# Strassen's identity in the first expert layer of the last two token chunks

## The chip, the cores and the metric

The kernel runs on one core of a Trainium2 chip. Its engines work side by side, each through its own queue of instructions in the order in which the program issues them: TensorE (PE: matmuls, with its weight loads listed as PEld), VectorE (DVE), ScalarE (ACT), GpSimd (POOL) and SyncE (SP, which only issues transfers). Engines wait for each other through semaphores. The metric is the device time of one execution in microseconds (us); lower is better. The time is a median over runs; the profile is of one further execution.

## The reference

An attention over 8 batches and 8 heads (576 queries of 64 numbers, and 16 beacon keys ahead of the 576 keys) is followed by a two-layer network on all 8 x 576 = 4608 tokens:

```python
scores = scale * np.matmul(q, k_all.transpose(0, 1, 3, 2))
scores = np.where(causal, -1000000000.0, scores)
a = np.exp(scores - scores.max(-1, keepdims=True))
a /= a.sum(-1, keepdims=True) + 1e-09
attn = np.matmul(a, v_all)
x = np.ascontiguousarray(attn.transpose(0, 2, 1, 3)).reshape(B * S, H * D)   # 4608 x 512
h = x @ w_in                      # 512 x 2048
g = np.maximum(0.01 * h, h)
out = (g @ w_out).astype(np.float32)   # 2048 x 512
```

## The kernel before

All instructions of the five engines stand in the order in which the Python code issues them (`tc.manual_schedule`); the framework adds the semaphore waits that the data and the buffers need.

**Attention.** Work goes by groups `g`, one for each pair of heads of a batch: 32 of them. A group has score matmuls (`score`, `stretch`, L314), exponentials on ACT (L329, L333), triangular masks on POOL (L289), value matmuls in two halves (`value`, L359), and a division on DVE (L388, L389) into `x_nat`. For groups 8 and on `x_turn` (L412) then issues transposes on SP's queue, which carry `x_nat` into `xT`, the tokens laid out with their 512 features over partitions. In the last batch `x_turn` issues three of them: L417, L422 and, last, L425 with the first 112 tokens of the batch. `xT` holds four batches at a time.

**The two layers.** Tokens go by chunks of 512, nine of them (`NCH`). Chunk 7 takes most of its tokens from batch 6 and its last 64 from batch 7; chunk 8 is all of batch 7. `moe1` computes 128 columns of the first layer for a chunk: four matmuls of 512 columns (L442) and one ACT instruction that applies the leaky ReLU into `gT` (L450). `up` does that once and keeps the count `done1`; there are 16 for a chunk.

The second layer already uses Strassen's identity in Winograd's form, on halves of the tokens, of the hidden features and of the output columns: seven products in the order `PRODUCTS = (1, 4, 6, 2, 7, 5, 3)`, each over two tiles of 128 tokens. `moe2` (L524) is one such tile, called a group here: 8 matmuls of 256 columns (L537). `down` does one group and keeps `at2` and `done2`; there are 14 for a chunk. `combine` (L556) puts the products together: products 1, 4 and 5 are copied from the bank by ACT (L568), the others are added by DVE (L565), and four blocks are stored by SP (L595). The sums of `gT` that the identity needs are made by DVE from `token_sums` (L469): two slices with four sums each. They wait in the list `due`, and `up` and `down` take one from it each time (`add_due`, L620).

**Order.** While attention runs, a list of `events` with due times places the attention's steps, and `fill` places `up` and `down` between them so that the work at hand is spread evenly up to the end of a batch; `KEPT` = 4 units are kept back. After the last event the loop at L836 runs what is left: the rest of chunk 6's groups, then all of chunk 7's first layer, then chunk 8's first layer and chunk 7's groups by turns, then chunk 8's 14 groups.

**PSUM.** The eight banks are divided into a pool of four single ones (`ps_one`, used by `moe1`, `moe2`, the value matmuls and a third of the score tiles) and a pool of two pairs (`ps_sc`, used by score tiles alone).

The step that matters for the change in the first layer is this:

```python
acc = ps_one.tile([128, 512], FP32, name="acc", tag="one")
...
nc.scalar.activation(out=gT[i][:, fc, :], in_=acc, func=AF.Prelu, alpha=0.01)
```

## Time and profile before

| | |
|---|---|
| runs | 326.14 us median of 3 (325.81 to 326.32) |
| profiled execution | 325.23 us, of it span 323.5 us |
| granted TensorE clock | 0.999 |
| PE busy | 317.3 us |
| DVE busy | 146.1 us |
| ACT busy | 199.3 us |
| first-layer matmuls (L442) | 640 recorded, 135.7 us |
| end of the last value matmuls | 257.6 us |
| chunk 7's first layer | 268.1 to 281.9 us |
| chunks 8 and 7 by turns | 281.9 to 308.0 us |
| chunk 8's second layer | 308.0 to 320.2 us |

The span runs from the program's first to its last recorded instruction; the rest of the execution's time lies around it. A line of the timeline gives the start and the length in us, the engine, the line of the kernel, the operation with its output and input, how many instructions were merged, and in brackets how long the engine was idle before and what ended that. Merged matmuls overlap, so their length is not their count times one. A line of the chain of work gives start, length, engine, tile and line.

### The profile page before, as it was taken

The page shows a single profiled execution, that of the slowest core. Times are in us where ns is not written, and L with a number is a line of the kernel's source. Part 1 is how long each engine was busy: PE and PEld are TensorE (multiplying, and loading weights), DVE is VectorE, ACT ScalarE, POOL GpSimd, SP SyncE. Part 2 cuts the span into 40 slices and gives each one's busy share as a digit, 9 for nine tenths or more (in the row PEclk, how much of TensorE's full clock was granted, in tenths as well). Part 3 has the DMA queues.
Part 4 walks back from the last instruction along what each step waited for, and adds up shares of the span by engine and source line. Part 5 has one row for each costly group of instructions (what it writes and reads, how often), then busy time and mean ns, then how long its engine had stood idle before and what let it go on. Part 6 is the DMA issues. An engine that isn't in the chain of part 4 may idle for free.

```text
span 323.5 us, 8521 instructions
## 1 busy us (share of the span) xinstructions
PE 317.3 (98%) x3429; PEld 213.4 (66%) x3429; DVE 146.1 (45%) x297; ACT 199.3 (62%) x336; POOL 184.7 (57%) x354
## 2 busy tenths in 40 slices
PE   8999999999999999999999999999999999999995
PEld 5574565445687558845888888656865785466684
DVE  3473354518446145434552455345444542325444
ACT  4969862487765786478647873786468415653420
POOL 8895968999997687659875977664221000000000
PEclk9999999999999999999999999999999999999999
DMA  8999999999999999999999999999112112000203
GB/s 140 137 206 175 147 214 120 188 165 190 157 138 169 218 147 107 124 174 80 154 192 160 110 127 115 196 128 135 52 53 79 24 54 97 2 1 32 79 20 132
DMA packets 155928, 39.93 MB, mean 123 GB/s; under 512 B 143040, under 2 KB 153152, under 8 KB 155888
## 3 DMA queue, kind: packets, MB, share of 16 engines
q0 software_dynamic: 99824, 18.54, 91.3%
q1 hardware_dynamic: 55792, 20.77, 37.1%
q8 instruction: 27, 0.44, 0.6%
q14 instruction: 13, 0.11, 0.1%
q10 hardware_dynamic: 272, 0.07, 0.1%
HBM read 37.22 MB, written 9.44 MB: 144 GB/s over the span
## 4 chain that ended last, share of the span: by engine, by line
PE 77%; DMA 10%; POOL 5%; ACT 3%; DVE 2%; issue 2%; DVEq 0%; POOLq 0%; ACTq 0%
PE acc L442 31%; PE acc L537 30%; PE av L359 6%; PE sc L314 6%; DMA w_out_sb<-in_moe_w_out_dram 4%; PE acc L512 4%; DMA w_in_sb<-in_moe_w_in_dram 4%; POOL aT L289 2%; DMA gsum<-in_k_dram 2%; ACT aT L333 2%; POOL gsum L158 2%; ACT aT L329 1%; DVE p L565 0%; ACT gT L450 0%; DVE u L565 0%
## 5 line engine op out<-in xcount | busy, mean ns | idle before, releaser
L442 PE MATMUL acc<-xT,w_in_sb 128*128 128x512 bf16 (+1 forms) x640 | 135.7, 358 | 0.3 <-ACT aT L329 0.3
L450 ACT ACTIVATE gT<-acc 128x512 bf16<-128x512 f32 x144 | 82.8, 621 | 46.4 <-PE acc L442 46.2
L442 PEld LDWEIGHTS <-w_in_sb 128*128 128x128 bf16 x640 | 59.6, 98 | 52.4 <-issue 2.9
L289 POOL TENSOR_SCALAR_AFFINE_SELECT aT<-aT 128x256 bf16<-128x256 bf16 (+2 forms) x160 | 59.7, 404 | 51.7 <-ACT aT L329 30.9
L537 PEld LDWEIGHTS <-gT 128*128 128x128 bf16 x512 | 48.8, 98 | 9.1 <-issue 1.8
L333 ACT ACTIVATE aT<-sc 128x1024 bf16<-128x1024 f32 (+3 forms) x64 | 51.8, 895 | 0.0
L537 PE MATMUL acc<-w_out_sb,gT 128*128 128x256 bf16 x384 | 46.2, 273 | 0.4 <-ACT gT L450 0.4
L329 ACT ACTIVATE aT<-sc 128x512 bf16<-128x512 f32 (+3 forms) x64 | 29.0, 522 | 27.9 <-PE sc L314 27.7
L388 DVE RECIPROCAL rec<-av 128x6 f32<-128x6 f32 (+1 forms) x64 | 12.0, 188 | 67.0 <-PE av L359 66.3
L359 PEld LDWEIGHTS <-aT 128*128 128x128 bf16 (+1 forms) x960 | 36.7, 98 | 8.3 <-issue 0.6
L537 PEld LDWEIGHTS <-gsum 128*128 128x128 bf16 x384 | 36.5, 98 | 6.2 <-issue 0.4
L359 PE MATMUL av<-v_aug,aT 128*128 128x65 bf16 (+1 forms) x960 | 39.4, 194 | 0.3 <-ACT gT L450 0.2
L214 POOL DMA_DIRECT2D v_aug<-in_v_dram x40 | 34.2, 859 | 4.1 <-DMA w_in_sb<-in_moe_w_in_dram 3.4
L568 ACT COPY p<-acc 128x512 f32<-128x512 f32 (+1 forms) x25 | 14.5, 580 | 35.6 <-PE acc L537 35.6
L171 POOL DMA_DIRECT2D k_nat<-in_k_dram x48 | 34.9, 733 | 1.3 <-DMA w_out_sb<-in_moe_w_out_dram 0.6
L171 POOL DMA_DIRECT2D q_nat<-in_q_dram x48 | 34.8, 731 | 0.6 <-issue 0.3
L389 DVE TENSOR_TENSOR x_nat<-av,rec 128x384 bf16<-128x384 f32 (+1 forms) x64 | 31.4, 491 | 2.2
L537 PE MATMUL acc<-w_sum,gsum 128*128 128x256 bf16 x256 | 31.9, 273 | 0.0
L276 ACT ACTIVATE aT<-sc 128x1024 bf16<-128x1024 f32 (+3 forms) x32 | 25.9, 875 | 3.5 <-PE sc L267 3.5
L620 DVE TENSOR_TENSOR gsum<-gT 128x1024 bf16<-128x1024 bf16 x16 | 11.0, 688 | 28.1 <-ACT gT L450 28.1
L314 PE MATMUL sc<-qT,kT 64*128 64x80 bf16 (+22 forms) x384 | 22.0, 250 | 0.3
L314 PEld LDWEIGHTS <-kT 64*128 64x128 bf16 x384 | 12.9, 94 | 10.9 <-issue 7.6
(62 smaller groups left out, 227.3 us busy)
## 6 DMA issues: line engine op xcount, KB each, us to landing
out_dram<-p SPq DMA_DIRECT2D x26, 256.0 KB, 3.2
q_nat<-in_q_dram POOLq DMA_DIRECT2D x48, 72.0 KB, 5.5
k_nat<-in_k_dram POOLq DMA_DIRECT2D x48, 72.0 KB, 5.0
v_aug<-in_v_dram POOLq DMA_DIRECT2D x24, 128.0 KB, 6.1
w_in_sb<-in_moe_w_in_dram POOLq DMA_DIRECT2D x2, 1024.0 KB, 11.7
w_out_sb<-in_moe_w_out_dram POOLq DMA_DIRECT2D x2, 1024.0 KB, 11.7
out_dram<-u SPq DMA_DIRECT2D x8, 256.0 KB, 2.7
gsum<-in_q_dram POOLq DMA_DIRECT2D x8, 144.0 KB, 6.9
```

Source lines behind the costliest of these rows:

```text
L171: nc.gpsimd.dma_start(out=t[:, :, par], in_=(q, k)[which][b, 2 * hp + par].rearrange("(t p) d -> p t d", p=NR),)
L214: nc.gpsimd.dma_start(out=dst[lo : ROWS[c], c, :, 0:D], in_=v[b, :, OFF[c] : OFF[c] + n].rearrange("h p d -> p h d"),)
L276: nc.scalar.activation(out=aT[:, :, c0 : c0 + w], in_=sc[:, :, 0:w], func=AF.Exp, scale=0.125)
L289: nc.gpsimd.affine_select(out=view, in_=view, compare_op=ALU.is_ge, fill=0.0, base=128 - n if lo == 0 else 0, channel_multiplier=-1, patte ...
L314: nc.tensor.matmul(out=(sc[par] if apart else sc[:, par])[:, at : at + b - a], lhsT=kT[ps_, c * 128 : (c + 1) * 128], rhs=qT[ps_, q0 : q0 ...
L329: nc.scalar.activation(out=probs[g][:, par, lo:hi], in_=sc[par][:, at : at + hi - lo], func=AF.Exp, scale=0.125)
L333: nc.scalar.activation(out=probs[g][:, :, lo:hi], in_=sc[:, :, at : at + hi - lo], func=AF.Exp, scale=0.125)
L359: nc.tensor.matmul(out=avv[:, n, 0 : D + 1], lhsT=aT[0 : ROWS[c], par, a0 : a0 + 128], rhs=va[0 : ROWS[c], c, 2 * hp + par, :], start=(c = ...
L389: nc.vector.tensor_tensor(out=x_nat[:, t0:t1].rearrange("p t e d -> p (t e) d"), in0=avv[:, :, 0:D], in1=rec[:, n0:n1, None].to_broadcast( ...
L442: nc.tensor.matmul(out=acc[:, lo:hi], lhsT=w_in_cols(fc, j), rhs=xT[:, j, x0 : x0 + hi - lo], start=(j == 0), stop=(j == NJ - 1), skip_gro ...
L450: nc.scalar.activation(out=gT[i][:, fc, :], in_=acc, func=AF.Prelu, alpha=0.01)
L537: nc.tensor.matmul(out=acc[:, lo : lo + HD], lhsT=left(i, n, fc, tile), rhs=right(n, fc), start=(lo == 0 and fc == 0), stop=(fc == HF - 1) ...
```

## The change

In the last two chunks (7 and 8) three quarters of the first layer are computed with the same identity: tokens, features and hidden columns are halved, and the 12 column blocks are taken in three rounds (`ROUNDS`), each of four blocks. A round (`in_round`) is seven products in the order 1, 4, 6, 5, 2, 7, 3, each of four matmuls of 256 columns; it takes the four banks of `ps_one`. Product 2 accumulates on product 1's bank, 7 on 6's, 3 on 5's, after the earlier product has been read: product 1 by an ACT copy into `p1`, product 6 by DVE's addition `u2`, product 5 by an ACT copy into `p5`. DVE then adds `u3`, `c21`, `c12` and `c22`, and the function `leave` inside the round is the ACT instruction that applies the leaky ReLU, from a bank for the first block and from SBUF for the other three. The remaining four column blocks of each chunk are done by `up` as before.

The sums of weights (`w_in_sums`, eight DVE instructions in all) and of tokens (`x_in_sums`, four for a chunk) go through `due`. They and the partial results lie in buffers that attention has finished with: `a_bufs`, the keys' buffer `k_all`, and part of `w_in_sb`.

The order changes too. The last group's `finish` comes one unit earlier, and `LEFT` = 14 groups of chunk 6 are kept back instead of 4 units, so that none of them is done before the last value matmuls. After the events stands an order written by hand (`last_chunks`: d a group, r a round, u a plain block, a that many entries of `due`, x the sums of a chunk's tokens put into `due`, t the same for the first slice of `gT`): seven groups of chunk 6 come before the first round, and single groups or pairs between the rounds. There the second layer takes its banks from `ps_sc` (one of each pair) instead of `ps_one`.

```diff
@@ -450,6 +450,13 @@
         nc.scalar.activation(out=gT[i][:, fc, :], in_=acc, func=AF.Prelu, alpha=0.01)
 
     HF, HD, HT = NF // 2, DM // 2, 256
+    TAIL, ROUNDS = NCH - 2, 3
+    apart_from_values = [False]
+
+    def one_bank():
+        if apart_from_values[0]:
+            return ps_sc.tile([128, 2, 512], FP32, name="sc", tag="sc")[:, 0]
+        return ps_one.tile([128, 512], FP32, name="acc", tag="one")
     ADD, SUB = ALU.add, ALU.subtract
 
     def weight_sums(part):
@@ -530,7 +537,7 @@
         n, tile = PRODUCTS[n2 // 2], n2 % 2
         apart = i == NCH - 1 and n2 >= 10
         if tile == 0 or apart:
-            banks["p"] = ps_one.tile([128, 512], FP32, name="acc", tag="one")
+            banks["p"] = one_bank()
         acc = banks["p"]
         lo = 0 if apart else tile * HD
         for fc in range(HF):
@@ -597,6 +604,122 @@
             in_=c.rearrange("p (t d) -> p t d", t=n),
         )
 
+    flat_a = [t.rearrange("p e c -> p (e c)") for t in a_bufs]
+    flat_k = k_all.rearrange("p n c -> p (n c)")
+    W_COLS, X_COLS, T_COLS = 2 * 256 * ROUNDS, 2 * HT, 1024
+    w_t = {n: flat_a[i][:, 0:W_COLS].rearrange("p (j f) -> p j f", j=2) for i, n in enumerate((5, 6, 4))}
+    w_t[7] = w_in_sb[1][:, 0:2, 0 : W_COLS // 2]
+    sum_at = [(i, W_COLS + n * X_COLS) for i in range(3) for n in range(3)]
+    temp_at = [(flat_k, n * T_COLS) for n in range(5)] + [(flat_a[3], n * T_COLS) for n in (1, 2)]
+    temps = {
+        name: t[:, lo : lo + T_COLS].bitcast(FP32)
+        for name, (t, lo) in zip(("p1", "p5", "u2", "u3", "c12", "c21", "c22"), temp_at)
+    }
+
+    def w_in_sums(n):
+        (b11, b21), (b12, b22) = (
+            [w_in_sb[i][:, lo : lo + 2, 0 : W_COLS // 2] for lo in (0, 2)] for i in range(2)
+        )
+        x, y = {5: (b12, b11), 6: (b22, w_t[5]), 4: (b21, w_t[6]), 7: (b22, b12)}[n]
+        due.extend((TAIL - 1, dict(out=w_t[n][:, j], in0=x[:, j], in1=y[:, j], op=SUB)) for j in range(2))
+
+    def x_parts(i):
+        at = i * 512 % (XR * S)
+        assert at + 512 <= XR * S
+        return [[xT[:, 2 * c : 2 * c + 2, at + r * HT : at + (r + 1) * HT] for c in range(2)] for r in range(2)]
+
+    x_sums = {}
+
+    def x_in_sums(i):
+        (a11, a12), (a21, a22) = x_parts(i)
+        s1, s2, s3, s4 = (
+            flat_a[t][:, lo : lo + X_COLS].rearrange("p (j t) -> p j t", j=2)
+            for t, lo in sum_at[4 * (i - TAIL) : 4 * (i - TAIL) + 4]
+        )
+        x_sums[i] = {5: s1, 6: s2, 7: s3, 3: s4}
+        return [
+            (i, dict(out=s1, in0=a21, in1=a22, op=ADD)),
+            (i, dict(out=s2, in0=s1, in1=a11, op=SUB)),
+            (i, dict(out=s4, in0=a12, in1=s2, op=SUB)),
+            (i, dict(out=s3, in0=a11, in1=a21, op=SUB)),
+        ]
+
+    def in_product(i, n, r, bank, first):
+        (a11, a12), (_, a22) = x_parts(i)
+        x = {1: a11, 2: a12, 4: a22}.get(n)
+        x = x_sums[i][n] if x is None else x
+        for f in range(2):
+            cols = slice(r * 256 + f, r * 256 + f + 255, 2)
+            for j in range(2):
+                if n in w_t:
+                    w = w_t[n][:, j, cols]
+                else:
+                    i0, j0 = {1: (0, 0), 2: (0, 2), 3: (1, 2)}[n]
+                    w = w_in_sb[i0][:, j0 + j, cols]
+                nc.tensor.matmul(
+                    out=bank[:, f * HT : (f + 1) * HT],
+                    lhsT=w,
+                    rhs=x[:, j],
+                    start=first and f == 0 and j == 0,
+                    stop=j == 1,
+                    skip_group_check=True,
+                )
+
+    def in_round(i, r):
+        if i not in gT:
+            gT[i] = gpool.tile([128, NF, 512], BF16, name="gT")
+        b = [ps_one.tile([128, 512], FP32, name="acc", tag="one") for _ in range(4)]
+        add = nc.vector.tensor_tensor
+
+        def leave(half, cols, src):
+            fc = cols * HF + 2 * r
+            nc.scalar.activation(
+                out=gT[i][:, fc : fc + 2, half * HT : (half + 1) * HT],
+                in_=src.rearrange("p (f t) -> p f t", f=2),
+                func=AF.Prelu,
+                alpha=0.01,
+            )
+
+        in_product(i, 1, r, b[0], True)
+        nc.scalar.copy(out=temps["p1"], in_=b[0])
+        in_product(i, 4, r, b[3], True)
+        in_product(i, 6, r, b[1], True)
+        add(out=temps["u2"], in0=b[1], in1=temps["p1"], op=ADD)
+        in_product(i, 5, r, b[2], True)
+        nc.scalar.copy(out=temps["p5"], in_=b[2])
+        in_product(i, 2, r, b[0], False)
+        leave(0, 0, b[0])
+        in_product(i, 7, r, b[1], False)
+        add(out=temps["u3"], in0=b[1], in1=temps["p1"], op=ADD)
+        add(out=temps["c21"], in0=b[3], in1=temps["u3"], op=ADD)
+        leave(1, 0, temps["c21"])
+        in_product(i, 3, r, b[2], False)
+        add(out=temps["c12"], in0=b[2], in1=temps["u2"], op=ADD)
+        leave(0, 1, temps["c12"])
+        add(out=temps["c22"], in0=temps["u3"], in1=temps["p5"], op=ADD)
+        leave(1, 1, temps["c22"])
+        done1[0] += 4
+
+    def last_chunks(steps):
+        for step in steps.split():
+            op, n = step[0], int(step[1:] or 1)
+            i = done1[0] // NF
+            if op == "d":
+                for _ in range(n):
+                    down()
+            elif op == "u":
+                for _ in range(n):
+                    up()
+            elif op == "r":
+                for _ in range(n):
+                    in_round(i, done1[0] % NF // 4)
+            elif op == "x":
+                due.extend(x_in_sums(n))
+            elif op == "a":
+                add_due(n)
+            elif op == "t":
+                due.extend((i, op) for op in token_sums(i, 0, SLICE))
+
     done1, done2, at2, ready, turn, first_down, held = [0], [0], [0, 0], [0], [0], [0], [0]
 
     def fill(rest=False):
@@ -671,7 +794,7 @@
             )
 
     NG = B * NPAIR
-    KEPT, LEAD = 4, 4
+    KEPT, LEAD, LEFT = 4, 4, 14
 
     def has(g):
         return 0 <= g < NG
@@ -811,9 +934,12 @@
             events.append((FIRST + (0.4 if m else 0.6) + 1536 / COLS * m, 2, block, (m,)))
         ends = [FIRST]
         for g in range(FIRST, NG):
-            events.append((g + 3.5, 2, finish, (g, 2)))
+            at = g + (2.5 if g == NG - 1 else 3.5)
+            events.append((at, 2, finish, (g, 2)))
             if g % NPAIR == NPAIR - 1:
-                ends.append(g + 3.5)
+                ends.append(at)
+        for at, n in ((NG - 1.2, 5), (NG - 0.3, 6), (NG + 0.7, 4)):
+            events.append((at, 7, w_in_sums, (n,)))
         for b in range(2, B):
             for n in range(2 if b == 2 else 0, NKB):
                 events.append((4 * b + ((-0.1, 0.1)[n > 3] if b == 2 else 0.3 * n - 0.4), 6, load_v_cast, (b, n)))
@@ -823,7 +949,7 @@
         for at, _, what, args in events:
             while w + 2 < len(ends) and at > ends[w + 1]:
                 w, d0 = w + 1, done1[0] + done2[0]
-            todo = NF * ready[0] + sum(ND(i) for i in range(ready[0])) - KEPT - d0
+            todo = NF * ready[0] + sum(ND(i) for i in range(ready[0])) - (KEPT if w + 2 < len(ends) else LEFT) - d0
             aim = d0 + todo * (at - ends[w]) / (ends[w + 1] - ends[w])
             while done1[0] + done2[0] < aim and fill():
                 pass
@@ -833,8 +959,12 @@
                 while done1[0] + done2[0] < since + (2 if has_down() else 4) and fill(True):
                     pass
             what(*args)
-        while at2[0] < NCH:
-            fill()
+        assert at2 == [TAIL - 1, ND(TAIL - 1) - LEFT] and done1[0] == TAIL * NF, (at2, done1)
+        apart_from_values[0] = True
+        w_in_sums(7)
+        due.extend(x_in_sums(TAIL))
+        last_chunks("d7 a9 r d2 x8 r d2 t r d1 u4 d2")
+        last_chunks("d2 a9 r d2 r d2 t r d2 u4 d6 d14")
 
 
 # ---- launch: one core; inputs and outputs as the reference has them ----
```

## The prediction

> **What bounds the kernel now.** I read the page's busy line first, then the chain of work that ended last in order of time, then the timeline of the last 75 us, then the groups by shape. The page:
>
> ```profile
> PE 317.3 (98%) x3429; PEld 213.4 (66%) x3429; DVE 146.1 (45%) x297; ACT 199.3 (62%) x336; POOL 184.7 (57%) x354
> ```
>
> TensorE (PE) is busy for 317.3 of 323.5 us. The chain, in order of time, shows the part that the change rewrites:
>
> ```profile
> 257.64 10.48 PE acc L537 x96
> 268.12 13.81 PE acc L442 x64
> ...
> 307.97 8.75 PE acc L537 x80
> 316.74 0.70 DVE u L565
> ```
>
> From 257.64 to 316.74 it is on PE without a break: nothing else counts while PE never waits. The rows price a matmul: 10.48 / 96 = 109.2 ns for 256 columns, 13.81 / 64 = 215.8 ns for 512. What else is needed comes from the timeline:
>
> ```profile
> 266.41 0.58 ACT L568 COPY p<-acc 128x512 f32<-128x512 f32 x1 [6.40 <-PE acc L537]
> 267.03 0.69 DVE L565 TENSOR_TENSOR u<-u,p 128x512 f32<-128x512 f32 x1 [0.89 <-ACT p L568]
> 267.75 0.69 DVE L565 TENSOR_TENSOR p<-u,p 128x512 f32<-128x512 f32 x1
> ...
> 276.42 0.69 DVE L620 TENSOR_TENSOR gsum<-gsum,gT 128x1024 bf16<-128x1024 bf16 x1
> 277.03 0.68 DVE L620 TENSOR_TENSOR gT<-gT 128x1024 bf16<-128x1024 bf16 x1
> 277.63 0.69 DVE L620 TENSOR_TENSOR gsum<-gT,gsum 128x1024 bf16<-128x1024 bf16 x1
> ...
> 286.12 1.03 PE L442 MATMUL acc<-xT,w_in_sb 128*128 128x512 bf16 x4
> 286.76 0.97 PEld L537 LDWEIGHTS <-gT 128*128 128x128 bf16 x8
> 286.98 1.04 PE L537 MATMUL acc<-w_sum,gT 128*128 128x256 bf16 x8
> 287.18 0.60 ACT L450 ACTIVATE gT<-acc 128x512 bf16<-128x512 f32 x1 [1.14 <-PE acc L442]
> ```
>
> A VectorE (DVE) addition follows one whose result it needs 0.72 us after (267.03 to 267.75), one that it does not need 0.61 after (276.42, 277.03, 277.63). A reader of a bank starts 0.20 us after PE's last matmul there has made way for the next group (286.98 to 287.18). ScalarE (ACT) hands over 0.04 after its end (266.99 to 267.03). Back to back, ACT takes 0.51:
>
> ```profile
> 245.55 2.12 ACT L450 ACTIVATE gT<-acc 128x512 bf16<-128x512 f32 x4
> ```
>
> (2.12 - 0.60) / 3. From SBUF in float32 the groups by shape have one row:
>
> ```profile
> L760 ACT CAST k_nat<-gsum 64x576 bf16<-64x576 f32 x1 | 0.7, 672 | 0.2 <-DMA gsum<-in_k_dram 0.2
> ```
>
> Scaled to 512 elements that is about 0.62, so a leave from SBUF costs what one from PSUM does. Last, the transposes into xT of the last pair of heads:
>
> ```profile
> 258.34 1.20 SPq L417 DMA_TRANSPOSE xT<-x_nat  x1
> 259.59 1.24 SPq L422 DMA_TRANSPOSE xT<-x_nat  x1
> 260.87 1.74 SPq L425 DMA_TRANSPOSE xT<-x_nat  x1
> ```
>
> ```profile
> DMA to landing us min/median/max: 2.3/2.4/2.9
> ```
>
> The second fence is the answer for L425. The third transpose carries the 64 tokens that chunk 7 lacks; it is issued 3.4 us after the last value matmul (257.5) and lands 2.3 to 2.9 later. Before, 12.2 us of groups stood ahead of chunk 7, so it hid.
>
> [...]
>
> **The change part by part.** *Removed:* in six rounds, 16 matmuls of 512 columns (3.45 us) give way to 28 of 256 (3.06 us): 0.40 each, **2.4 us off PE**. The 14 groups of the second layer per chunk are as many as before.
>
> *Added on DVE and ACT:* per round five float32 additions (u2, u3, c21, c12, c22) in place of none, and six ACT instructions in place of four. A chunk then has 22 float32 additions and 8 sums of gT at 0.61 and 4 sums of x at 0.34, some 19.7 us of DVE against 3 x 3.06 + 3.45 + 14 x 0.874 = 24.9 us of PE. ACT has 18 + 4 + 3 at 0.51, 12.8 us. Load alone costs nothing; what costs is order, because PE now returns to banks that DVE or ACT must have read. Products 2, 7 and 3 accumulate where 1, 6 and 5 lie: product 2 waits for the copy of product 1 (ACT), product 7 for u2 (DVE), which itself needs that copy.
>
> *Standard case* (round 1 to 2 of chunk 7), from the end of product 7 of the earlier round. DVE: u3 0.20, c21 0.92, c12 1.53, c22 2.14, seen 0.72 later at 2.86. ACT's queue is in order, so the new round's copy of product 1 stands behind the leave of c22: leave 2.86, copy 3.37, done 3.99. PE meanwhile does product 3 (0.44), two groups (1.75) and products 1, 4, 6, 5 (1.75), and wants product 2 at 3.93: late 0.06. u2 runs 3.99 to 4.71; PE wants product 7 at 4.37: **late 0.34** in all.
>
> *Round 2 to 3, chunk 7:* behind c22 DVE has a sum of x (2.75), the second layer's u (3.09) and p (3.81), another sum (4.42), then u2 at 4.76, ready 5.48 against 4.37: **1.11**.
>
> *Round 3 to chunk 8's round 1:* c22 2.14, two sums of x to 3.43. The next addition needs the copy of p5, which stands in ACT's queue behind the leave of c22: 3.37, done 3.99. From there two additions (3.99, 4.71), four sums of gT (5.32, 6.04, 6.65, 7.26), then 7.87, the product 3 addition 8.48, sums 9.09, 9.70, 10.31, u2 10.92, ready 11.64. PE: product 3 0.44, a group 0.87, four plain columns 3.45, four groups 3.49, five products 2.18, product 7 at 10.43: **1.21**.
>
> *Chunk 8, round 1 to 2:* the second layer's copy of p4 stands ahead of the copy of product 1 on ACT: done 4.50, product 2 late 0.57, u2 ready 5.22: **0.85**. *Round 2 to 3:* standard, **0.34**.
>
> *Chunk 7, round 1* is moved up: seven groups (6.1 us) stand between the last value matmul and it. The third transpose lands at 5.8 to 6.3 after that matmul; the first sum of x waits for it on DVE, with the second layer's u2 and three sums queued behind it: sum 5.9, u2 6.24, sum 6.85, seen at 7.31; PE wants product 6 at 6.99, late 0.32, and product 7 another 0.1: **0.4**, or 0.9 with the late landing.
>
> *At nothing:* the eight sums of w_in run under attention and the first groups (0.55 us each, estimated as for x), with DVE at 45%; two banks for the second layer instead of four suffice, since a pair of groups lasts 1.75 us and its reader 0.20 + 0.7; uncovered, the last four single groups could lose 0.05. Later stores on SP hold nobody until the last, whose tail after PE (additions, store) is unchanged.
>
> *Sum:* 0.4 + 0.34 + 1.11 + 1.21 + 0.85 + 0.34 = 4.25 of new waits, less 2.41 = **+1.8**, rounded to +1.9 with the last banks. The profiled execution took 325.23 us with a span of 323.5; its span would become 325.4. The median of the runs is 0.9 above that execution: 326.14 + 1.9 = **328.0 us**.
>
> **Bounds of what the trace does not show.** Sums of 512 bfloat16: 0.2 to 0.5 spacing, four on PE's path, -0.5 to +0.6; I take 0.34. Leave from SBUF: 0.60 to 0.67, +0.3 at most. Weights loaded from every second column under a matmul of 256: L442 loads such columns only under 512; its loads average 98 ns, like L537's contiguous ones, which do fit in 109. Zero is taken, 20 ns each on 168 matmuls (3.4 us) is the upper end. A gain below nothing has no source there.
>
> **Rivals.** *(a) Faster:* DVE drains its queue sooner than 0.61 per addition. About 32 additions and sums stand in the chains above, so 2.0 us of waiting less, 0.06 each (0.55 spacing), makes the change even, and 0.085 makes it 0.65 faster; with no waits at all 323.7. For it: DVE's total of 19.7 fits in 24.9. Against: each spacing is measured on the same shapes. *(b) No change:* half the waits go, the two long ones at chunk 8's start and round 3 being met by slack in sums that are off the path: 326.1. *(c) Much slower:* alternate-column weight loads or a late landing add 2 us or more: 330 to 332. Against: the 98 ns. That the change does not save its 2.4 is excluded by the counts of matmuls.
>
> **How the numbers follow.** My forecast, 326.8 to 329.5, gets 0.62; (c) 0.14; (b) 0.10; (a) 0.14. Runs of before spread over 0.5 us, so 0.2% (0.65 us) is about what can be told from nothing: faster 0.14, same 0.10, slower 0.76. The range reaches down to 325.4, past (b), and up to 330.0, some way into (c), leaving out about 2 in 10.
>
> **What would show it.** PE idle of 4 to 5 us between the last value matmul and the end, ended by DVE's u2 and ACT's copy at products 7 and 2, longest (about 1.2) at chunk 8's first round and chunk 7's third; product matmuls at 109 ns. DVE nearly without gaps from c22 to u2 there. Wrong would be: no such idle (a), matmuls slower than 109 ns (c), or product 4 waiting for a transpose by over 1 us.

## The result, and the profile after

The changed kernel took 330.11 us in the median of six runs, the kernel before 325.83; the ratio is 1.0123, with a 95% interval of 1.0084 to 1.0161. In a second series beside the experiments it was 329.53 against 326.33, a ratio of 1.0088 (1.0057 to 1.0120). It is slower, by 3 to 4 us. Medians are over all runs; the ratios leave out the runs in a slower state that either kernel shows now and then, one of these six. The profiled execution took 330.05 us with a span of 328.1. The busy line of its page:

```profile
PE 316.4 (96%) x3501; PEld 220.0 (67%) x3501; DVE 170.2 (52%) x343; ACT 204.7 (62%) x348; POOL 185.7 (57%) x354
```

TensorE (PE) is busy 0.9 us less than before and the span is 4.6 us longer; DVE has 46 instructions and 24 us more. The waits between 245 us and the end (columns: who waited for whom, total us, times, longest us) name the causes:

```profile
DVE aT L743 <- DMA xT<-x_nat: 3.1, 1, 3.1
...
PE acc L659 <- DVE kT L687: 1.9, 2, 1.0
...
PE acc L659 <- DVE aT L743: 0.9, 1, 0.9
...
PE acc L659 <- DMA xT<-x_nat: 0.6, 1, 0.6
...
PE acc L659 <- ACT kT L684: 0.4, 1, 0.4
```

L659 is a product's matmul, L687 is u2, L684 the copy of product 1, L743 a sum that was due. The chain that ended last (start, us, what) ran on PE without a break before. Now it comes to the first round of chunk 7 by way of the transposes and DVE:

```profile
258.92 1.23 SPq L422
260.15 0.04 issue
260.19 4.02 DMA xT<-x_nat
...
264.58 0.68 DVE u L572
265.26 0.34 DVE aT L743
265.61 0.04 issue
265.65 2.06 PE acc L659 x16
```

It is the third transpose, 4.02 us under way; its view by source line has this answer:

```profile
DMA to landing us min/median/max: 2.3/2.4/4.0
```

Before, the same line read 2.3/2.4/2.9. The timeline at that place and at the three longest seams behind it:

```profile
263.35 0.27 PE L659 MATMUL acc<-xT,aT 128*128 128x256 bf16 x1
...
264.24 0.43 DVE L743 TENSOR_TENSOR aT<-xT 128x512 bf16<-128x512 bf16 x1 [3.13 <-DMA xT<-x_nat]
264.26 0.49 PE L659 MATMUL acc<-xT,aT 128*128 128x256 bf16 x3 [0.63 <-DMA xT<-x_nat]
...
265.65 0.60 PE L659 MATMUL acc<-aT,aT 128*128 128x256 bf16 x4 [0.91 <-DVE aT L743]
...
278.23 1.03 PE L659 MATMUL acc<-aT,w_in_sb 128*128 128x256 bf16 x8 [0.86 <-DVE kT L687]
...
290.26 1.03 PE L659 MATMUL acc<-aT,w_in_sb 128*128 128x256 bf16 x8 [0.99 <-DVE kT L687]
...
295.19 0.60 PE L659 MATMUL acc<-xT,w_in_sb 128*128 128x256 bf16 x4 [0.40 <-ACT kT L684]
```

The brackets are the idle time that a releaser ended, counted to the modelled end of the last matmul; the first matmul of a row keeps its slot of 109 ns, so I take a wait from start to start, less 109 ns for each matmul between. In round 1 that is 0.80 us at product 4, which waits for the landing (263.35 to 264.26), 1.06 at product 6, which waits for a sum of x, and 0.14 at product 7. By site, beside the forecast and a second execution of the same kernel (a1 below), in us:

| Site | Forecast | After | After, again |
|---|---|---|---|
| Chunk 7, round 1 | 0.4 | 2.00 | 0.34 |
| Chunk 7, round 1 to 2 | 0.34 | 0.43 | 0.43 |
| Chunk 7, round 2 to 3 | 1.11 | 1.11 | 1.10 |
| Round 3 to chunk 8 | 1.21 | 1.16 | 1.16 |
| Chunk 8, round 1 to 2 | 0.85 | 0.85 | 0.85 |
| Chunk 8, round 2 to 3 | 0.34 | 0.36 | 0.36 |
| Last banks | 0.05 | 0.07 | 0.07 |
| Sum | 4.30 | 5.98 | 4.31 |

**The start-up.** Of the 4.6 us between the two spans, 1.0 us lies ahead of any changed instruction. One group of 18 value matmuls, ahead of the tail in every kernel, serves as a mark. In PE's timelines of the kernel before, the same kernel again (b1 below), and the changed one:

```profile
236.84 0.72 PE L359 MATMUL av<-v_aug,aT 128*128 128x65 bf16 x18
```

```profile
239.06 0.72 PE L359 MATMUL av<-v_aug,aT 128*128 128x65 bf16 x18
```

```profile
237.85 0.72 PE L359 MATMUL av<-v_aug,aT 128*128 128x65 bf16 x18
```

Two executions of one and the same program reach the mark 2.2 us apart, so 1.0 us there says nothing about the change. From here on I use the time from the mark to the end of the span, which leaves the start-up out: 86.66 before, 90.25 after. The difference, 3.6 us, is 5.98 of waits less the 2.41 of saved TensorE work. (The views give the span to 0.1 us, so each of these times can be off by 0.05.)

### The profile page after: what moved, and what is told of

It reads as the page before. It is cut to its first block, busy times and chain, and to the rows that moved or that the text cites. A ratio compares the mean times of both kernels' runs of the same rounds, so it can differ in the third digit from the quotient of the medians.

```text
span 328.1 us, 8750 instructions
## 1 busy us (share of the span) xinstructions
PE 316.4 (96%) x3501; PEld 220.0 (67%) x3501; DVE 170.2 (52%) x343; ACT 204.7 (62%) x348; POOL 185.7 (57%) x354
## 4 chain that ended last, share of the span: by engine, by line
PE 76%; DVE 8%; ACT 6%; DMA 4%; POOL 3%; issue 2%; SPq 1%; ACTq 0%; POOLq 0%; DVEq 0%
PE acc L442 29%; PE acc L544 19%; PE av L359 9%; PE sc L544 6%; PE sc L314 6%; PE acc L519 3%; DMA v_aug<-in_v_dram 3%; PE acc L659 2%; ACT aT L333 2%; DVE gsum L743 1%; ACT gT L676 1%; PE sc L267 1%; DMA xT<-x_nat 1%; POOL gsum L158 1%; POOL v_aug L214 1%
## 5 line engine op out<-in xcount | busy, mean ns | idle before, releaser
L442 PE MATMUL acc<-xT,w_in_sb 128*128 128x512 bf16 (+1 forms) x544 | 113.0, 354 | 0.7 <-ACT aT L276 0.4
L289 POOL TENSOR_SCALAR_AFFINE_SELECT aT<-aT 128x256 bf16<-128x256 bf16 (+2 forms) x160 | 60.6, 408 | 50.6 <-ACT aT L329 30.8
L450 ACT ACTIVATE gT<-acc 128x512 bf16<-128x512 f32 x120 | 68.1, 625 | 28.1 <-PE acc L442 27.9
L442 PEld LDWEIGHTS <-w_in_sb 128*128 128x128 bf16 x544 | 50.1, 98 | 44.2 <-issue 3.5
L544 PE MATMUL acc<-w_out_sb,gT 128*128 128x256 bf16 x240 | 28.9, 273 | 0.4 <-ACT gT L450 0.4
L544 PE MATMUL acc<-w_sum,gsum 128*128 128x256 bf16 x160 | 20.1, 273 | 0.0
L575 ACT COPY p<-acc 128x512 f32<-128x512 f32 x15 | 9.1, 604 | 16.8 <-PE acc L544 16.8
L743 DVE TENSOR_TENSOR gsum<-gT 128x1024 bf16<-128x1024 bf16 x16 | 11.0, 688 | 15.3 <-ACT gT L450 15.3
```

Of the source, the lines that this page charges most:

```text
L289: nc.gpsimd.affine_select(out=view, in_=view, compare_op=ALU.is_ge, fill=0.0, base=128 - n if lo == 0 else 0, channel_multiplier=-1, patte ...
L442: nc.tensor.matmul(out=acc[:, lo:hi], lhsT=w_in_cols(fc, j), rhs=xT[:, j, x0 : x0 + hi - lo], start=(j == 0), stop=(j == NJ - 1), skip_gro ...
L544: nc.tensor.matmul(out=acc[:, lo : lo + HD], lhsT=left(i, n, fc, tile), rhs=right(n, fc), start=(lo == 0 and fc == 0), stop=(fc == HF - 1) ...
```

## The experiments

My theory: the matmuls saved are real and the loss is waits, each set by the order of the queues of DVE and ScalarE, with the landing of the third transpose on top. Rivals: the rearrangement itself costs; the start-up does; DVE is simply full. The waits of all runs below are taken from start to start, as in the table.

**e1, the order alone.** Each Strassen round gives way to four plain blocks; groups ahead, separate banks and order stay.

```diff
-        w_in_sums(7)
-        due.extend(x_in_sums(TAIL))
-        last_chunks("d7 a9 r d2 x8 r d2 t r d1 u4 d2")
-        last_chunks("d2 a9 r d2 r d2 t r d2 u4 d6 d14")
+        last_chunks("d7 a9 u4 d2 u4 d2 u4 d1 u4 d2")
+        last_chunks("d2 a9 u4 d2 u4 d2 u4 d2 u4 d6 d14")
```

(The earlier sums of w_in are left out too.)

> The order of the changed kernel kept (seven second-layer groups ahead, value banks apart), but each Strassen round replaced by four plain first-layer blocks, and no sums of weights or of x. My theory (the loss is the waits of the rounds, 6.0 us, less 2.4 us of TensorE work saved): TensorE work is that of the kernel before, and the only wait in the tail is the first plain block of chunk 7 for the third transpose, 1.3 us if it lands as late as in the changed kernel (4.0 us after issue), 0 if it lands after 2.4 us; so 0 to 1.3 us over the kernel before in the profiled execution. Rival (the rearrangement itself, pools apart and groups moved ahead, costs what was lost): 3 to 4 us over the kernel before, with waits at the places of the order and not of the sums. Start-up theory (the 1.0 us of extra idle time before 80 us is scatter of an execution): it is there or not there without regard to the tail.

Measured: 86.82 us from mark to end, level with the 86.66 and 86.74 of the two profiles of before; PE waits 0.07 us in the tail, at the last banks, and the view of waits has no row of PE there. The rearrangement costs nothing in the tail; what is lost belongs to the rounds. The transpose landed 2.4 us after issue here, to which I come back. In 18 runs against 52 the ratio is 1.0026 (1.0006 to 1.0046), some 0.8 us that this profile's tail does not show; its mark stood 0.34 us late. That remainder is not explained.

**a1 and b1, both kernels again.** No edit.

> The changed kernel once more, beside the others. My theory: the waits in the tail behind round 1 are the same to 0.05 us (0.43, 1.11, 1.16, 0.85, 0.36), since they come from queues; the landing of the third transpose is late again, since TensorE's fetches fall at the same instruction, and round 1 of chunk 7 waits 1.5 to 2.0 us. The 1.0 us of the start-up is scatter of an execution: it may be anything from 0 to 2 us here. Rival (the start-up belongs to this program): it is 1.0 us again to within 0.2.

> The kernel before, profiled once more, for the start-up alone: if its starts of the value matmuls from 80 us on differ from those of its first profile by 0.5 us or more, the 1.0 us between the two kernels ahead of the changed part is scatter; if they agree within 0.1 us, it isn't. Its tail has no wait of TensorE either way, and the ratio is 1 within its interval.

Measured: the mark moves by 2.2 us between two executions of before, so the start-up is scatter (the ratio of before to itself is 0.9996, 0.9975 to 1.0017); for the changed kernel it was 0.8 late. The seams of the changed kernel repeat to 0.01 us, as the table shows. One expectation failed: the transpose was not late. The waits of this execution have neither a PE row for the transpose nor one for a sum:

```profile
PE acc L659 <- DVE kT L687: 1.9, 2, 1.0
DVE aT L743 <- DMA xT<-x_nat: 1.5, 1, 1.5
...
PE acc L659 <- ACT kT L684: 0.4, 1, 0.4
```

Round 1 waits 0.34 where I had worked out 0.4, the waits sum to 4.31 against 4.30, and mark to end is 88.57, 1.9 us over before: the forecast's sum, in an execution where its landing holds. So what makes the landing late?

**e2, e8 and e9, the fetches of TensorE's own instructions.** A queue with the kind "instruction" carries 27 packets of 16,384 B in the span, one to 259 of TensorE's 7,002 matmuls and weight loads; I take them for TensorE's, one to 256 instructions, and the three runs test it. In the changed kernel one lies inside the flight of the third transpose. The DMA view from its issue to its landing:

```profile
q1 hardware_dynamic: 248, 0.05, 5.8%
q8 instruction: 1, 0.02, 1.4%
```

Its record starts at 262.20, 2.01 us after the issue, and takes 0.92 us; by 262.56, 15 of the 16 completions of the transpose are in, the last comes at 264.21. The three runs shift the packet with unused matmuls in the start-up, whose results are not read; w64.16 is the edit of e2, e8 has w128.16 in its place and e9 w32.16. e8 and e9 are one execution each (339.78 and 330.42 us), of which the tail alone is read.

```diff
-        run("v2.0 V1.0 V1.1 q4 v2.1 x1 k4.1 v3.0 v3.1 x2.1 s4.0 s4.1 x3 m4.0 V1.2 V1.3 V1.4 l7.0 l7.1 u u s4.2 s4.3 q5 k5 m4.1 m4.2 u o0 u")
+        run("v2.0 V1.0 V1.1 q4 v2.1 x1 k4.1 v3.0 v3.1 x2.1 s4.0 s4.1 x3 m4.0 V1.2 V1.3 V1.4 l7.0 l7.1 w64.16 u u s4.2 s4.3 q5 k5 m4.1 m4.2 u o0 u")
```

> The changed kernel with 64 unused matmuls added where TensorE stands idle in the start-up, so that TensorE's own instruction fetches (packets of 16,384 B, one in 256 of its instructions) fall 128 instructions, some 7 us, away from the third transpose of x of chunk 7. My theory (one of the sixteen parts of that transpose stands behind such a packet): it lands 2.3 to 2.4 us after its issue instead of 4.0, the waits of round 1 of chunk 7 fall from 2.0 to about 0.4 us, and the span by 1.6 us; the other sites keep their waits (0.43, 1.11, 1.16, 0.85, 0.36). Rival (the transpose is late for another reason, such as stores or the queue it stands in): landing stays at 4.0 and the wait at 2.0 us. The 64 matmuls themselves cost nothing if the idle time covers them, at most 64 x 0.06 = 4 us if not.

> The changed kernel with 128 unused matmuls in the start-up (256 instructions of TensorE with their weight loads, so one fetch of 16,384 B more and the later ones back where they were against the work). My theory (a fetch in flight together with the third transpose makes it late): the packet lies again some 2 us behind the issue of the transpose, which lands 3.9 to 4.3 us after its issue, as in five of the seven runs that had the packet there; round 1 of chunk 7 waits 1.5 to 2.3 us. Rival (late landings come and go by themselves): no relation to the packet. The unused matmuls cost up to 8 us ahead of the tail; the tail alone is read.

> The same with 32 unused matmuls (64 instructions, a quarter of a fetch's distance): the packet lies some 2.6 us sooner, half a microsecond ahead of the issue of the third transpose, where it can only be in the way of the second. My theory: the third lands 2.3 to 2.9 us after issue, round 1 of chunk 7 waits 0.3 to 0.9 us. Rival (as above): 3.9 us or more is as likely as before.

In e2 the same view from issue to landing has no packet of instructions:

```profile
q1 hardware_dynamic: 247, 0.05, 9.7%
```

It landed after 2.4 us, round 1 waited 0.35 us, the other seams stayed (0.43, 1.10, 1.15, 0.85, 0.36): mark to end 88.55, as in a1. The matmuls were not hidden: the mark stood 4.5 us later than before and 3.5 later than in after, 0.05 to 0.07 us for each of the 64, and the ratio is 1.018. In e8, with 256 instructions more than in after, the packet came 1.87 us after the issue again (2.01 in after), and the transpose was late again:

```profile
DMA to landing us min/median/max: 2.3/2.4/4.2
```

Round 1 waited 2.22 us, mark to end 90.45. In e9 I missed: the transpose landed after 2.4 us, but round 1 waited 1.19. The packet (at 260.16) had met the second transpose while SP was issuing it, and the third stood behind it:

```profile
258.82 1.20 SPq L417 DMA_TRANSPOSE xT<-x_nat  x1
260.07 2.07 SPq L422 DMA_TRANSPOSE xT<-x_nat  x1
262.19 1.23 SPq L425 DMA_TRANSPOSE xT<-x_nat  x1
```

The issue took 2.07 us instead of 1.23, the third came 0.84 later, and the time was lost all the same. Over all profiles with a tail of the changed order, when the packet started after the issue of the third transpose, and its landing, in us:

| | after | e3 | e4 | e5 | e6 | e8 | e1 | a1 | e7 | e5 again | e2 | e9 |
|---|---|---|---|---|---|---|---|---|---|---|---|---|
| Packet | 2.01 | 1.91 | 1.93 | 1.91 | 1.91 | 1.87 | 2.24 | 2.33 | 2.32 | 2.30 | -4.22 | -2.03 |
| Landing | 4.0 | 4.3 | 3.9 | 4.3 | 4.2 | 4.2 | 2.4 | 2.4 | 2.4 | 2.4 | 2.4 | 2.4 |

Where nothing is in the way, the last packet of the transpose ends 2.04 us after the issue. In the six profiles in which a fetch starts before that, while the transpose is still moving, the last packet ends between 2.9 and 3.2; in the other six nothing of this transpose is held. The six and the six fall apart without exception. The limit of 2.04 us is that of this transpose, not a rule: in e2 an earlier one (L422, issued at 257.17) had its last packet by 2.15 us and yet landed after 4.2, with a fetch that started at 2.31. What one packet holds back is one sixteenth, as the DMA records of after show: of the transpose's last 32 packets, 4 B each, 30 have ended by 262.23, and the other two start at 263.10 and 263.11, while the packet of instructions ends at 263.12 (262.20 and 0.92 us). The last of the 16 completions, 1.65 us behind the other 15, is the landing.

**e3, the last Prelu of a round behind the copy.** On ScalarE, c22's Prelu waits for the next round's copy of product 1.

```diff
         nc.scalar.copy(out=temps["p1"], in_=b[0])
+        while held_leave:
+            held_leave.pop()()
...
-        leave(1, 1, temps["c22"])
+        held_leave.append(lambda: leave(1, 1, temps["c22"]))
+        if r == ROUNDS - 1:
+            held_leave.pop()()
```

> The changed kernel with one thing moved on ScalarE: the Prelu of c22, the last of a round, is issued behind the next round's copy of product 1 and not ahead of it (in a chunk's third round at once, as before). My theory (the waits at the seams between rounds come from DVE's last sums of the round, then ScalarE's Prelu behind them in its queue, then the copy of product 1 that the next round's sums need): the waits go from 0.43 to about 0.06 (chunk 7, round 1 to 2), from 0.85 to 0.28 (chunk 8, round 1 to 2) and from 0.36 to 0.06 (chunk 8, round 2 to 3); 1.11 (chunk 7, round 2 to 3) and 1.16 (round 3 to chunk 8), which DVE's due sums set, stay within 0.1. Together 1.3 us less than the changed kernel. Rival (ScalarE isn't in that chain, DVE alone is): the product-1 waits stay and the time is within 0.3 us of the changed kernel.

Measured, with PE's rows of the waits in the tail:

```profile
PE acc L659 <- DVE kT L691: 1.9, 2, 1.0
PE acc L659 <- DVE aT L749: 0.9, 1, 0.9
PE acc L659 <- DMA xT<-x_nat: 0.9, 1, 0.9
```

The row for ScalarE's copy is gone. By site 0.43 became 0.13, 0.85 became 0.25, 0.36 became 0.13; 1.11 and 1.16 are 1.10 and 1.15. That is 1.13 us less where 1.3 were expected, 0.07 too little at the two short seams. The tail as a whole is 89.37, 0.9 less than after (the landing was late here too, at 4.3); the ratio to before is 1.0054 (1.0032 to 1.0077), half of what the change costs.

**e6, the due sums on GpSimd.**

```diff
             elif op == "a":
                 add_due(n)
+                due_on[0] = nc.gpsimd
...
     def add_due(n=1):
         while due and n:
-            nc.vector.tensor_tensor(**due.pop(0)[1])
+            due_on[0].tensor_tensor(**due.pop(0)[1])
```

(The sums up to the `a9` of chunk 7 stay on DVE.)

> The changed kernel with the due sums of the tail behind the first ones of x (those of x of chunk 8 and the token sums of chunks 7 and 8) on GpSimd, which has nothing to do there, in place of DVE. My theory (those sums, queued ahead of DVE's work in the next round, make the waits at chunk 7 round 2 to 3, 1.11 us, and at round 3 to chunk 8, 1.16 us): both fall below 0.4 us, those of 0.43, 0.85 and 0.36, which have no due sums in front but ScalarE's Prelu, stay within 0.15; if GpSimd is 2 or 3 times slower than DVE's 0.61 us for a 128x1024 sum, up to 2 us come back where chunk 7's sums are first read, at its fifth group. Rival (DVE's sums of the round set these waits, not the due ones): 1.11 and 1.16 stay. A second rival (the two engines hinder each other): DVE's own additions take longer than 0.69 us while GpSimd sums.

Measured: 337.97 us, a ratio of 1.0343 (1.0298 to 1.0387). The two waits that my theory puts down to due sums fell, from 1.11 to 0.43 and from 1.16 to 0.14, so the cause is right. As a remedy it is the worst of those tried. The groups by shape in the tail (busy us, mean ns):

```profile
L744 POOL TENSOR_TENSOR gsum<-gT 128x1024 bf16<-128x1024 bf16 x4 | 9.4, 2348 | 16.1 <-ACT gT L676 15.4 <-ACT gT L450 0.7
```

```profile
L699 DVE TENSOR_TENSOR aT<-kT 128x512 f32<-128x512 f32 x6 | 8.6, 1429 | 0.0
...
L694 DVE TENSOR_TENSOR aT<-acc,kT 128x512 f32<-128x512 f32 x6 | 4.2, 692 | 0.3
```

GpSimd takes 2,348 ns in the mean for a sum that takes DVE 686; of its sixteen such sums the shortest took 2,119, 3.1 times as long, the longest 2,576. And c22 (L699), with both operands in SBUF, grew on DVE from 681 to 1,429 ns in the mean, while c21 (L694), with one operand in PSUM, kept its 692. The second layer's additions from SBUF alone (L572, p from u and p) grew from 692 to 1,635. So such additions take longer while GpSimd sums, as the second rival had it; what ties them to each other, and what makes the longer sums on GpSimd longer, is not shown. The new waits (2.25 us at chunk 8, round 1 to 2, and 3.40 in the last groups) come from there, and round 1 of chunk 7, with slower sums besides a late landing, waits 3.35.

**e4, the due sums in the gap.** DVE has nothing to do inside a round between u2 and u3. The sums are issued there, c22's Prelu is held as in e3, and nine groups stand ahead of chunk 7. In the order, `r2` is now one round with two sums in its gap.

```diff
-    def in_round(i, r):
+    def in_round(i, r, gap=0):
...
         add(out=temps["u2"], in0=b[1], in1=temps["p1"], op=ADD)
+        add_due(gap)
...
-        last_chunks("d7 a9 r d2 x8 r d2 t r d1 u4 d2")
-        last_chunks("d2 a9 r d2 r d2 t r d2 u4 d6 d14")
+        last_chunks("d9 a9 r2 d2 x8 r2 d2 r2 t d1 u4")
+        last_chunks("d4 r1 d2 r1 d2 t r1 d2 u4 d4 d14")
```

> The changed kernel with the Prelu of c22 held as in the run before this, the due sums (of weights, of x, of the next chunk's tokens) issued in DVE's gap inside a round, behind u2, instead of at its end, and nine second-layer groups ahead of chunk 7 instead of seven. My theory (each wait is DVE's or ScalarE's queue or the landing): nine groups end 7.9 us behind the last value matmul, the transpose has landed by 7.4, so round 1 of chunk 7 waits under 0.3 us; waits in the tail 1.3 us in all (0.48 at chunk 7 round 1 to 2, 0.38 in round 3, about 0.06 at each other seam) instead of 6.0; with 2.4 us of TensorE work saved, 1.0 us under the kernel before, or level with it if the 1.0 us at the start-up belongs to every kernel with this tail. Rival (DVE has no room for the sums, wherever they stand): waits of 4 us or more and 1.5 us or more over the kernel before.

Measured: mark to end 87.22; 326.91 us, a ratio of 1.0021 (0.9997 to 1.0045). The waits are 2.98 us in all: behind round 1 they are as expected (0.49 and at most 0.26), so DVE has room. Expected in all were 1.3 us, though: the nine groups did not cover a late landing (3.9), which cost 1.42 us:

```profile
265.16 0.43 DVE L750 TENSOR_TENSOR aT<-xT 128x512 bf16<-128x512 bf16 x1 [3.02 <-DMA xT<-x_nat]
265.50 0.68 DVE L572 TENSOR_TENSOR u<-sc,p 128x512 f32<-128x512 f32 x1
...
266.24 1.03 PE L544 MATMUL sc<-w_out_sb,gT 128*128 128x256 bf16 x8 [1.26 <-DVE u L572]
```

PE doesn't need the sum yet. It needs the bank that u empties, and u stands on DVE behind the sum that waits.

**e5, u ahead of the sum.**

```diff
-        due.extend(x_in_sums(TAIL))
-        last_chunks("d9 a9 r2 d2 x8 r2 d2 r2 t d1 u4")
+        last_chunks("d6 x7 d3 a9 r2 d2 x8 r2 d2 r2 t d1 u4")
```

> The run with due sums in the gap, with one thing more: the sums of x of chunk 7 go onto DVE behind the second layer's addition of product 6 and not ahead of it. In the run before, the transpose landed 3.9 us after issue; DVE stood 3.0 us in the first of those sums, the addition u behind it in DVE's queue, and TensorE's ninth group 1.42 us for the bank that u empties. My theory (a late landing costs by what is queued behind it on DVE): the 1.42 us go even if the landing stays late, the other waits stay (0.49, 0.26, about 0.14 at each seam, 0.19), 1.5 us in the tail in all; in the median 1.4 us under that run and about 0.8 us under the kernel before. Rival (TensorE needs the sums themselves as soon, so the wait moves to product 6 or 5 of round 1): the tail stays within 0.3 us of 3.0 us.

> The run with the sums behind u once more, since its first ratio, 0.9986 (0.9970 to 1.0001), left open whether it is faster than the kernel before. From its tail (1.9 us of waits against 2.4 us of TensorE work saved) it should be 0.5 us or 0.15% under the kernel before: a ratio of 0.997 to 1.0. If the tail was only a lucky execution, the ratio is 1.002 or more, as for the other two runs with due sums in the gap.

Measured, in the first of the two, where the transpose landed after 4.3 us:

```profile
261.19 0.69 DVE L572 TENSOR_TENSOR u<-sc,p 128x512 f32<-128x512 f32 x1 [1.20 <-PE sc L544]
263.40 0.43 DVE L750 TENSOR_TENSOR aT<-xT 128x512 bf16<-128x512 bf16 x1 [1.52 <-DMA xT<-x_nat]
263.54 0.60 PE L659 MATMUL acc<-xT,w_in_sb 128*128 128x256 bf16 x4
```

u is done before the landing, PE runs through its groups into round 1, and the 1.42 us are gone; 0.49 remains at product 7, which waits for u2. The waits are 1.91 us in all, mark to end 86.16; in the second, with the landing in time, 1.58 and 85.89. Against 86.66 before that is 0.5 and 0.8 us less, the saved 2.41 less the waits. In the medians 325.92 against 326.33, and 326.54 against 326.89: ratios of 0.9986 (0.9970 to 1.0001) and 0.9985 (0.9962 to 1.0007). Both lie about 0.15% under the kernel before, and neither interval leaves 1 out: that this order is faster than before is not shown.

**e7, two additions more in the gap.** The second addition of product 7 of the second layer and the last two sums of x of chunk 7 go behind u2.

```diff
             add(part("u3", True), acc, part("u2"))
-            add(part("p4"), part("u3"), part("p4"))
-            store(i, 1, 0, tiles, part("p4"))
...
+            held_add.append(second)
...
         add_due(gap)
+        add_held()
...
-        last_chunks("d6 x7 d3 a9 r2 d2 x8 r2 d2 r2 t d1 u4")
+        last_chunks("d6 p7 d3 e r2 d2 x8 r2 d2 r2 t d1 u4")
```

(`second` is that addition with its store; `p7` puts two of the four sums of x into `due`, `e` the other two.)

> The run with the sums behind u, with two more things moved on DVE: the second addition of the second layer's product 7 (and its store) waits for the gap behind u2 of the next round, and the last two sums of x of chunk 7 for the gap of its first round. My theory (each wait of product 2 for u2 is the time of what stands ahead of u2 on DVE): the 0.50 us of chunk 7 round 1 to 2 fall to at most 0.1, the 0.49 of round 1 to at most 0.3; the other waits stay (0.26, about 0.13 at four seams, 0.19); some 1.2 us in the tail in all instead of 1.9, so 0.7 us under that run and about 1.2 us under the kernel before. Rival (the wait only moves on: product 7, which needs the third sum of x and the bank that u2 empties, or the groups behind the round wait instead): the tail within 0.2 us of 1.9.

Measured: round 1 to 2 of chunk 7 fell from 0.50 to 0.13, as expected, and the next seam rose from 0.26 to 0.87. Round 1 waits 0.47, at product 7 for the third sum of x, although the landing was in time; e5's second execution, in time too, has 0.14 there. The waits are 2.13 us, mark to end 86.41, the ratio 1.0012 (0.9984 to 1.0040): no better than e5. The rival was right: the wait moved on. The timeline at the risen seam:

```profile
276.55 0.68 DVE L718 TENSOR_TENSOR aT<-kT 128x512 f32<-128x512 f32 x1
276.67 0.63 ACT L691 ACTIVATE gT<-kT 128x512 bf16<-128x512 f32 x1
...
277.21 0.56 ACT L579 COPY p<-sc 128x512 f32<-128x512 f32 x1
...
277.67 0.59 ACT L699 COPY kT<-acc 128x512 f32<-128x512 f32 x1
...
278.31 0.60 PE L671 MATMUL acc<-xT,w_in_sb 128*128 128x256 bf16 x4 [0.41 <-ACT kT L699]
```

Three additions in the gap push u3, c21 and c12 behind it (c12 to 275.95), c12's Prelu later with them, then the two copies behind it on ScalarE, and product 2 waits for the second. Two additions fit into the gap, three do not.

## Why the prediction was half right

The forecast was 1.9 us over before, 328.0 us, in a range of 326.8 to 329.5; the two medians are 330.11 and 329.53.

**The direction and the mechanism: right.** PE waits where DVE's and ScalarE's queues hand a bank back too late, and the waits outweigh the work saved. The five seams and the last banks came within 0.09 us of the working, in both executions. e1 shows that without rounds no wait is left; e3 takes away most of the waits that the working put down to ScalarE's Prelu (1.13 of 1.64 us), and of those alone; e6 and e4 those that it put down to the due sums.

**The saved work: right.** 88.57 - 86.66 = 1.9 in a1 is the 4.3 of waits less 2.4. Products run in 109 ns per matmul (the eight that start at 267.10 make way for the next group at 267.97), so weights from every second column cost nothing, the upper end of 3.4 us (an assumed 20 ns each) is out, and that part of rival (c) falls.

**The step that failed: chunk 7, round 1.** The mechanism was right, the term was mis-sized: 0.4 us was worked out, or 0.9 with a landing after 2.9; it was 2.00, with a landing after 4.0. Product 4 alone waited 0.80 us for the transpose, which the working had at nothing, and product 6 1.06 us for a sum of x behind it, which it had at 0.32. (The sign of being wrong that the prediction named for this, product 4 waiting over 1 us, appears in e3 and e8, at 1.06 and 1.02.) I took both ends of the landing from the five of one source line and thus took the worst case seen there for the worst there is. The view of the tile xT in the same profile (246 to 272 us, all three lines) has a longer one:

```profile
DMA to landing us min/median/max: 2.3/2.4/3.5
```

It is the second transpose of the same three, with a fetch 1.03 us after its issue. The 2.9 is the third, which met that fetch too (it started 0.25 us ahead of the third's issue, which took 1.74 us on SP instead of 1.22). So a longer landing than the worst case taken lay in the profile before, on a neighbouring line.

What the runs put in the place of 2.3 to 2.9 in the changed kernel: 2.4 us when no fetch of TensorE's instructions meets the transpose, 3.9 to 4.3 when one does. In the kernel before, nothing depends on such a delay: twelve groups, 96 matmuls in 10.5 us, stand between the value matmuls and chunk 7 (the 12.2 us of the prediction would be fourteen). The other half of rival (c), a late landing that adds about 2 us, is what the first series shows; a1 shows the forecast's own case. Which of them comes is a matter of 0.3 us in the packet's start. How often it comes in executions without a profile, no run shows. The second median, 3.2 us over before, lies between the 1.9 and the 3.6 of the two tails; the first, 4.3, needs some start-up on top, which its profile has.

**Rivals (a) and (b): wrong as to the changed kernel.** DVE's spacings are as measured before: 0.72 us to an addition that needs the one ahead of it (272.97 to 273.69 in after), 0.60 to one that does not (274.30 to 274.90). But that DVE has room for all its work was true, and e5 lives on it: with the same additions in another order (and two groups more ahead of chunk 7) the waits fall from 4.31 to 1.58 us where the landing is in time, and from 5.98 to 1.91 where it is late.

**Lengths taken as estimates: right.** The 0.34 us of spacing for a sum of x and the 0.55 us for a sum of w_in were estimates of mine. In the groups by shape of before, three bfloat16 sums of 128x2048 (L461 to L463) take 1,216 to 1,225 ns and those of 128x1024 (L620, gsum from gT) 688; in proportion that is about 0.42 us for 512 columns and 0.56 for 768. In after a sum of x takes 0.42 us, and the next addition starts 0.34 or 0.35 us behind one that it does not need (264.24 to 264.58, 265.63 to 265.98); the sums of w_in take 550 to 552 ns. A leave from SBUF takes 630 ns there, one from a bank 600 (L676), where the prediction had about 0.62 and 0.60.

**Small misses.** Round 1 to 2 of chunk 7 is 0.43, not 0.34: product 2 already waits 0.14 there, not 0.06. The start-up, which the sum took as equal, differed by 1.0 us, and the time around the span by 0.2 us; the 0.9 that the median of before stood above its profile covered most of it.

## What to carry to other kernels

When PE comes back to a bank within a few microseconds, count not the load of the reading engine but what stands ahead of the reader in its queue, sums that could wait included; put those into the engine's gaps, up to the size of the gap, and never queue an instruction that waits for a transfer ahead of one that frees a bank (in e4 that cost 1.42 us). A landing time read from a few transfers is a sample, not a bound: a transfer that comes onto the critical path should have cover for the delay that a packet in its way can cause, here 1.5 to 1.9 us. When a margin is under a microsecond, compare from a mark behind the start-up, which moved by 2.2 us here, and not whole spans.

## What the runs showed that I had not expected

- TensorE's instructions come by DMA beside the data: 27 packets of 16,384 B for 7,002 instructions, 0.92 to 1.78 us each in after, and one of them delays a transpose of 2.4 us by 1.5 to 1.9 us, or its issue on SP from 1.23 to 2.07 us.
- While GpSimd sums in e6, DVE additions from SBUF alone take up to 2.64 us (c22 at 305.70; 2.37 at 292.08) instead of 0.68; those with an operand in PSUM stay at 0.69.
- After the waits of 2.25 and 3.40 us in e6 the granted clock of PE fell; in the windows view (us, PE, PEld, DVE, ACT, POOL busy, clock, DMA share, GB/s):

```profile
296.00:300.00 4.00, 3.88 (x21) 2.77 (x21) 2.63 (x5) 1.68 (x4) 0.43 (x1) 0.57 0.01 4
```

Matmuls of 256 columns then stood 0.21 us apart instead of 0.109 for the next 3.4 us. Behind the second wait, of 3.40 us, the granted clock was 0.57 too (320 to 324 us). It fell after one of 2.13 us in e8's start-up as well (at 36.87; mean of that execution 0.989), but not after one of 1.69 in e4's (at 62.03; mean 1.0), nor after the waits of up to 1.4 us in the tails of the other runs; what length it takes between these, or whether it is one length, is not shown. So the wait of 2.25 us cost nearly twice that: with it came some 1.6 us of half clock.
